# The taps of two convolution blocks as trees of accumulating DMAs, in a fused convolution and gelu kernel on one core

## The chip, the core and the metric

The kernel runs on one core of a Trainium2 chip. A core has five engines that work side by side and wait for each other through semaphores: TensorE (PE in the profile; its weight loads are the row PEld), VectorE (DVE), ScalarE (ACT), GpSimd (POOL) and SyncE (SP, which here only issues DMAs). GpSimd issues DMAs too, on a queue of its own (q0); those can add what they carry to what lies at the destination (`accum_op`). The metric is the device time of one execution in microseconds. The kernel before took 2390.29, 2388.48 and 2389.80 us in three runs, median 2389.8.

## The reference

A lightweight convolution in front of a two-layer network, all in fp32, B = 8 sequences of S = 4096 tokens, D = 192 channels. The convolution is causal and has seven taps per head; each of 8 heads has 24 channels, and its taps go through a softmax:

```
w = softmax(weight, axis=-1)                     # (8 heads, 7 taps)
out[b,s,h,:] = sum over k of w[h,k] * x_pad[b, s+k, h,:]   # six zeros ahead of x
h = out.reshape(32768, 192) @ w_in               # 192 -> 2048
g = h * (1 / (1 + exp(-1.702 * h)))
return g @ w_out                                 # 2048 -> 192
```

## The kernel before

**Steps.** The 32768 tokens are worked in 32 steps (`big`, 0 to 31). A step has 512 tokens of a sequence p and the same 512 of the sequence p + 4, so 1024 tokens. Channels lie in three blocks of 64 (`c` = 0, 1, 2); the partitions of a block hold 64 channels of two stretches of 256 tokens. Step 0 is done plainly while the weights arrive (`first_step`, `second_first`). Every other step is three stages: `hidden(big, 0)`, `hidden(big, 1)` and `second(big)`. TensorE never changes from one step to the next until it is through with all three.

**First product.** `hidden` computes `h` for half of the features (v = 0 or 1) by a scheme of 21 products (`TERMS`) in place of 24, each of a weight sum in `w_in_s` with a sum of convolution blocks. Products gather in PSUM banks (`x`, `y`, `z` among the `slots`, and `sums`), ScalarE copies some out (`copy2`, L615), VectorE combines (`sum2`, L619), and ScalarE writes the gelu to `g` (L600, L604). The weight sums `SUMS_W` are made by VectorE at the start (`sums_w_in`), and TensorE's main loop is line L578.

The convolution blocks are called C11, C12 (block 0, for the two sequences), C21, C22 (block 1) and C31, C32 (block 2). Eight sums of them, V1 to V8 (`SUMS_C`), are made by GpSimd (`sums_c`); V1 = C31 - C11 is the first. Each half of the partitions also needs the other half's blocks, so the blocks and sums cross over by DMAs on SP's queue (`cross`, L507): V1 as soon as it is there (`"first big"`), since the last-but-one stage before a step already starts its first product with V1 (`fetch`), the rest piece by piece.

**Second product.** `second` multiplies the 16 blocks of `g` by `w_out`, by a scheme of 25 products of sums of blocks with sums of weights (`w_form`). The blocks lie in "spots" of 128x1024; eight accumulations between spots are done per step by VectorE or by GpSimd's DMAs (`"acc"`, L904, 512 KB each). The results, 96x256, are combined by VectorE ("joins", L387 and L389), turned by a transpose (L846) and stored. All of it follows one list, `PLAN`, written out by hand. Its items are issued in order, each on its engine's queue: `go n` is n groups of four matmuls (L928, some 0.43 us a group; 78 in all), `main f s to` names form f, spot s and the bank where the following groups gather, `side` a form whose matmuls run as every fourth, `seed` a ScalarE copy (L957) which puts a value into a bank ahead of products that add to it, `join`, `turn` and `store` the end of a result. After the last group the stage runs on into `hidden` of the next step.

**Convolution ahead.** The blocks of a step are made two steps earlier, in two strands:

- `prepare(big)` gives items with a price in us to the queue `todo`; a call `work(us)` in `hidden` or `second_first` issues as many as fit its price. Those of block 1 are seven VectorE instructions (`conv`, L484 and L486); behind them come the sums V1 to V8 and the crossings.
- `prepare_taps(big)` gives 14 items to the queue `ready`: blocks 0 and 2, seven taps each. The seven of block 0 are issued by `("tap",)` in `PLAN`, those of block 2 by `taps_at(n)` in the v = 0 stage of `hidden`. A tap is one ScalarE multiplication and, but for the first, one GpSimd addition:

```
act.mul(home, conv_src(big, c, k), cw[:, c, k : k + 1])     # L494
nc.gpsimd.tensor_add(dst, dst, home)                        # L496, if k > 0
```

The multiplication of tap 0 writes the block itself. The others write a `home` of 128x512; there are four, half-spots of spots 16 and 15 (`TAP_SPOTS`), used in turn by both blocks. For steps 1 and 2 block 0 uses other places, since the spots are still taken.

**Order on the queues.** GpSimd takes its instructions in order: tap additions, `sums_c`, the issue of accumulating DMAs (for the DMA itself it does not wait), and at the start the weight forms: `SUMS_O` in `second_first`, and four more, `SUMS_O_LATE`, which are issued with the ScalarE sign changes `TURN_O` (L433) by `end_forms` out of `todo`, at the latest ahead of the first `second`. ScalarE takes gelus, copies, seeds and tap multiplications in order, VectorE sums, joins, turns, convolutions and the transposes of x (L465). SP issues the input loads of x (eight per step), the crossings and the stores.

Of the kernel before, what the change touches and what calls it, by code (L numbers as in the profile page):

```python
# [11 lines left out]
ALU = mybir.AluOpType  # L12
# [3 lines left out]
def kernel(  # L16
# [29 lines left out]
    nc = tc.nc  # L46

    B, S, D = x.shape
    H, K = weight.shape
# [37 lines left out]
    def load_x(big, ns=range(2)):  # L87


        p, c = divmod(big, CHUNKS)  # L90
        if c == 0 and 0 in ns:
            (nc.gpsimd if big else vec).memset(xin[0:R, :, 0, :], 0.0)
        for n in ns:
            for o in range(2):
                j = 1 if c == 0 and o == 0 else 0
                t = c * TOK + o * T + (j - 1) * Q
                for v in range(2):
                    q0 = o * R + v * Q
                    nc.sync.dma_start(
                        out=xin[q0 : q0 + Q, n, j:NJ, :],  # L100
                        in_=x_v[n, p, t : t + (NJ - j) * Q, v * Q : v * Q + XW].rearrange(
                            "(j i) d -> i j d", i=Q
                        ),
                    )
# [15 lines left out]
    def block(r, j):  # L120

        return g[:, r, j // 2, j % 2, :, :]

    def row(n, i):
        return g[:, i // NG, n, :, i % NG, :]
# [13 lines left out]
    def spot(i):  # L139

        if i >= SPOTS:
            return block(*divmod(i - SPOTS, NG))
        flat = osbs[:, i * BLK : (i + 1) * BLK] if i < 2 else room[:, ROOMS[i - 2], :]
        return flat.rearrange("p (k t) -> p k t", k=NG)

    KEPT_LATE, TAP_SPOTS = 3, (16, 15)

    def kept(i):

# [26 lines left out]
    def own(big):  # L176
        return conv_t[:, big % 2 * 2, :, :]
# [41 lines left out]
    def form(i):  # L219

        if i < WHOLE:
            return w_out_s[:, i // NG, i % NG * NG : (i % NG + 1) * NG, :]
        return w_form[:, i - WHOLE, :, :]
# [9 lines left out]
    SUMS_O_LATE = [  # L233
        (23, 1, "+", 0), (24, 1, "+", 3), (1, 14, "+", 22), (7, 0, "-", 21),
    ]
# [73 lines left out]
    for c in range(NC):  # L309
        part = sel[:, c, :].rearrange("i (h q) -> i h q", h=2)  # L310
        for sign in (1, -1):
            nc.gpsimd.affine_select(
                out=part,
                in_=part,
# [70 lines left out]
    def add_up(v, dst, a, op, b, eng=vec):  # L385
        if op == "+":
            eng.tensor_add(v(dst), v(a), v(b))  # L387
        elif op == "-":
            eng.tensor_sub(v(dst), v(a), v(b))  # L389
        elif op == "n":  # L390
            vec.scalar_tensor_tensor(
                out=v(dst), in0=v(a), scalar=-1.0, in1=v(b), op0=ALU.mult, op1=ALU.subtract
            )
        else:
            vec.tensor_scalar_mul(v(dst), v(a), -1.0)
# [30 lines left out]
    def add_forms(items):  # L426
        for dst, a, op, b in items:
            add_up(form, dst, a, op, b, eng=nc.gpsimd)

    def end_forms():  # L430
        add_forms(SUMS_O_LATE)
        for i in TURN_O:
            act.mul(form(i), form(i), -1.0)  # L433

# [32 lines left out]
            xin[:, ns, :, :].rearrange("p n j d -> p (n j) d")[:, :, c * R : c * R + Q],  # L467
        )

    taps = [spot(i)[:, k : k + 2, :] for i in TAP_SPOTS for k in (0, 2)]  # L470
    first_taps = [row(0, k) for k in (2, 3, 6, 7)]

    def tap_home(big, c, k):
        return (first_taps if big < 3 and c == 0 else taps)[(3 * c + k - 1) % len(taps)]

    def conv_src(big, c, k, ns=slice(0, 2)):
        return xts[big][:, c, ns, Q - PAD + k : Q - PAD + k + T]

    def conv(big, c, k, ns=slice(0, 2), times=vec.tensor_scalar_mul):
# [5 lines left out]
        else:  # L485
            vec.scalar_tensor_tensor(  # L486
                out=dst, in0=src, scalar=tap, in1=dst, op0=ALU.mult, op1=ALU.add
            )

    def tap(big, c, k):  # L490

        dst = own(big)[:, 2 * c : 2 * c + 2, :]
        home = tap_home(big, c, k) if k else dst
        act.mul(home, conv_src(big, c, k), cw[:, c, k : k + 1])  # L494
        if k:
            nc.gpsimd.tensor_add(dst, dst, home)  # L496

    def sums_c(big, i):
        add_up(
            lambda j: own(big)[:, place(big, j), :],  # L500
            *SUMS_C[i],
            eng=vec if big == 1 else nc.gpsimd,
        )
# [34 lines left out]
    def give(early, big):  # L538
        given[early] = big
        for what in waiting[early]:  # L540
            cross_now(early, *what)
        waiting[early].clear()
# [44 lines left out]
    def terms(big, v, slot, *ts, first=False):  # L587
        for t in ts:
            product1(slot, *TERMS[t], big, v, first)
            first = False  # L590
# [22 lines left out]
    def copy2(dst, src):  # L613
        for h in range(2):
            act.copy(bank(dst, h), bank(src, h))  # L615
# [10 lines left out]
    def hidden(big, v, x, z, y, sums, work, fetch, last=lambda: None):  # L626

        def pe(slot, *ts, first=False):  # L630
            terms(big, v, slot, *ts, first=first)

        def taps_at(n):
            for _ in range(0 if v else n):
                next_tap()

        def early(i):
            for item in EARLY_G[i] if v else ():
                sum_g(*item)


        if v:
            pe(z, 7, first=True)
            give(True, big)
        if v:
            pe(sums, 12)
            copy2(k15, sums)
            pe(x, 5, 17)
        else:
            pe(x, 5)  # L650
            pe(sums, 12)
            copy2(k15, sums)
            pe(x, 17)
            taps_at(1)
        gelu(B11, 0, v, x)
        if not v:
            pe(z, 7, first=True)
        pe(sums, 0)
        taps_at(1)
        copy2(k16, sums)  # L660
        taps_at(2)
        last()
        def turn_next():
            if big + 2 < N_BIG:
                need(f"done {big + 1}")
                turn_x(big + 2)

        early(0)
        if big == 1:
            work(3.2 if v else 1.6)  # L670

        pe(y, 6, 14, first=True)
        sum2(vec.tensor_sub, x, z, k15)
        early(1)
        if not v or big == 1:
            work(1.2)
        pe(sums, 13)
        copy2(k19, sums)
        pe(x, 2)
        copy2(k18, x)  # L680
        taps_at(2)
        pe(z, 11)
        pe(sums, 20, 10)
        sum2(vec.tensor_sub, k15, y, k19)
        gelu(B12, 0, v, sums)
        pe(x, 4)
        copy2(k20, x)
        sum2(vec.tensor_sub, k19, z, k19)
        early(2)
        if not v or big == 1:  # L690
            work(1.1)
        gelu(B22, 1, v, k19)
        gelu(B22, 0, v, k15)
        taps_at(1)
        pe(y, 8)
        pe(sums, 1, 9, first=True)
        pe(y, 15)
        if v and big == 1:
            turn_next()
        elif not v:  # L700
            work(2.2 if big > 1 else 1.1)
        sum2(vec.tensor_add, k20, k20, sums)
        sum2(vec.tensor_sub, k16, y, k16)
        gelu(B11, 1, v, k20)
        pe(x, 18)
        gelu(B21, 1, v, x)
        early(3)
        fetch()
        if not v:

            copy2(y, z)
        gelu(B21, 0, v, k16)
        if not v:
            work(1.2)
        if not v and big > 1:
            turn_next()
        pe(sums, 3, 19)
        if not v:
            work(0.7)
        sum2(vec.tensor_add, k18, k18, sums)  # L720
        return lambda: gelu(B12, 1, v, k18)
# [127 lines left out]
    def store(big, n, o=None, queues=(nc.sync,) * 3):  # L849
# [32 lines left out]
        ("go", 1), ("cross",), ("acc", 18, 14), ("go", 1), ("seed", "p1", "k1", 1), ("sum", 5, 7, "+", 15),  # L882
        ("tap",), ("go", 2), ("main", 21, 7, "p2", 0), ("go", 1), ("sum", 6, 14, "+", 6), ("go", 1), ("tap",),
        ("side", 7, 20, "k1"), ("go", 2), ("sum", 6, 6, "-", 17), ("main", 10, 14, "p0", 0), ("go", 2),
        ("tap",), ("seed", "k5", "p2", 1), ("cross",), ("join", "k10", "k10", "+", "k8"), ("go", 2),
        ("join", "p2", "p4", "+", "k3"), ("main", 8, 8, "p1", 0, 0, 2), ("go", 1),
        ("join", "k8", "k9", "+", "k5"), ("tap",), ("go", 1), ("join", "k8", "k7", "-", "k8"),
        ("main", 4, 6, "p4", 0), ("go", 1), ("turn", 1, 0, 1, "k10"), ("go", 1),
# [3 lines left out]
        ("join", "k2", "k2", "-", "k1"), ("main", 12, 18, "p3", 0), ("go", 1), ("turn", 0, 0, 0, "k7"),  # L892
        ("go", 1), ("join", "k6", "k6", "+", "p4"), ("tap",), ("go", 1), ("turn", 1, 1, 1, "k2"), ("go", 1),
        ("turn", 1, 0, 0, "k6"), ("store", 0, 0), ("main", 24, 19, "p5", 0), ("go", 2), ("final",),
        ("join", "k1", "p3", "-", "k3"), ("go", 1), ("turn", 0, 0, 1, "k1"), ("store", 0, 1), ("go", 1),
        ("join", "k2", "p2", "-", "k4"), ("turn", 0, 1, 1, "k2"), ("store", 1, 1),
        ("join", "k1", "p5", "+", "k5"), ("turn", 0, 1, 0, "k1"), ("join", "k8", "k8", "+", "k0"),
        ("turn", 1, 1, 0, "k8"), ("store", 1, 0),
    ]
# [1 line left out]
    def sum_g(dst, a, op, b=None):  # L901

        if op == "acc":
            nc.gpsimd.dma_start(out=spot(dst), in_=spot(a), accum_op=ALU.add)  # L904
        else:
            add_up(spot, dst, a, op, b)
# [79 lines left out]
    def work(us):  # L986
        while todo and todo[0][1] <= us + 0.2:
            us -= todo[0][1]
            todo.pop(0)[2]()

    def next_tap():
        if ready:
            ready.pop(0)[2]()
            while ready and ready[0][1] == 0:
                ready.pop(0)[2]()
# [39 lines left out]
    def first_step(fetch):  # L1035
# [118 lines left out]
            fetch()  # L1154

        second_first(between)
        load_x(3)
        need("sums")

# [63 lines left out]
```

## Time and profile before

| what | us |
| --- | --- |
| three runs, median (lowest, highest) | 2389.8 (2388.48, 2390.29) |
| profiled execution | 2388.73 |
| its span, from the first to the last instruction | 2387.0 |
| granted TensorE clock, mean | 0.996 |
| busy: PE / DVE / ACT / POOL | 2302.0 / 2070.8 / 1545.0 / 892.7 |
| GpSimd's tap additions (L496), 360 of 1.360 | 489.5 |
| ScalarE's tap multiplications (L494), 420 | 301.7 |
| GpSimd's sums of convolution blocks, 240 | 209.6 |
| accumulating DMAs L904, 124 of 512 KB, median from issue to landing | 5.8 |

A line of the profile names a line of the kernel, an engine, an operation, and the tiles it writes and reads. A row of groups gives the instructions of one kind with their number, total and mean time, and what ended the idle time before them; the view of waits lists who waited for whom, with total, count and mean; the timeline lists single instructions with start and duration; the table of stretches gives the busy time of each engine between two moments. The chain that ended last, followed back from the last instruction, lies on PE for 83% of the span and on DVE for 9%.

### The profile page before, as it was taken

Reading aid. Unit: us, or ns where it says so; the run is one execution under the profiler, and the core shown is the slowest. Engines: PE = TensorE matmul, PEld = TensorE weight load, DVE = VectorE, ACT = ScalarE, POOL = GpSimd, SP = SyncE. Lnnn points to the kernel's source line nnn. Section 1 sums busy time; section 2 is a strip of 40 time slices with the busy share of each in tenths; the row PEclk is TensorE's granted clock in tenths of the full one; section 3 lists DMA queues with packets and bytes.
Section 4 is the critical chain, followed back from the end, with each engine's and each line's share of the span. In section 5 each row is a group of like instructions: output and inputs, shape, how many; then the busy total and the mean of one; then the engine's idle time right before and its main releaser. Section 6 shows DMA issues by size and latency. Waiting matters only on the chain.

```text
span 2387.0 us, 60716 instructions
## 1 busy us (share of the span) xinstructions
PE 2302.0 (96%) x25238; PEld 1347.5 (56%) x25238; DVE 2070.8 (87%) x2794; ACT 1545.0 (65%) x2942; POOL 892.7 (37%) x824
## 2 busy tenths in 40 slices
PE   9889999999999999999999999999999999999999
PEld 5365555555555555555555555555555555555556
DVE  8978888888888888888988888888888888888877
ACT  7356666667666676666676666766567666667654
POOL 0634442434433344333444233443334432344400
PEclk9999999999999999999999999999999999999999
DMA  7254345543455534455434555344553345542343
GB/s 179 59 116 89 77 91 121 106 106 80 87 105 108 120 79 84 94 117 111 96 79 86 117 108 112 83 86 95 110 119 86 79 91 121 108 103 60 71 94 68
DMA packets 239362, 232.59 MB, mean 97 GB/s; under 512 B 114672, under 2 KB 198512, under 8 KB 238960
## 3 DMA queue, kind: packets, MB, share of 16 engines
q1 hardware_dynamic: 210656, 130.80, 24.1%
q0 software_dynamic: 26784, 97.53, 21.7%
q8 instruction: 198, 3.24, 0.6%
q10 hardware_dynamic: 1648, 0.39, 0.1%
q14 instruction: 76, 0.62, 0.1%
HBM read 53.15 MB, written 25.17 MB: 33 GB/s over the span
## 4 chain that ended last, share of the span: by engine, by line
PE 83%; DVE 9%; ACT 2%; issue 0%; ACTq 0%
PE slot L578 32%; PE slot L928 26%; PE sums L578 15%; PE sums L928 10%; DVE room L389 5%; DVE room L387 3%; DVE osbs L846 1%; ACT g L494 1%; DVE slot L387 1%; ACT room L957 0%; ACT room L953 0%; ACT w_out_s L433 0%; ACTq L953 0%; ACT room L615 0%; ACT w_form L433 0%
## 5 line engine op out<-in xcount | busy, mean ns | idle before, releaser
L578 PE MATMUL slot<-conv_t,w_in_s 64*128 64x512 f32 x3740 | 957.0, 595 | 16.4 <-issue 8.8
L928 PE MATMUL slot<-g,w_form 128*32 128x256 f32 x7024 | 713.2, 379 | 0.0
L496 POOL TENSOR_TENSOR conv_t<-conv_t,g 128x512 f32<-128x512 f32 x360 | 489.5, 1360 | 563.6 <-ACT g L494 548.7
L578 PEld LDWEIGHTS slot<-conv_t,w_in_s 64*128 64x128 f32 x3740 | 499.1, 187 | 351.3 <-issue 230.0
L578 PE MATMUL sums<-conv_t,w_in_s 64*128 64x512 f32 x1660 | 496.4, 594 | 0.3 <-DVE w_in_s L372 0.3
L389 DVE TENSOR_TENSOR g<-g 128x1024 f32<-128x1024 f32 x372 | 448.7, 1234 | 3.9 <-ACT g L604 0.7
L928 PEld LDWEIGHTS slot<-g,w_form 128*32 128x32 f32 x7024 | 371.3, 110 | 119.6
L604 ACT ACTIVATE g<-room 128x1024 f32<-128x1024 f32 x310 | 324.3, 1073 | 106.0 <-DVE room L619 106.0
L953 ACT COPY room<-slot 32x256 f32<-32x256 f32 x434 | 159.0, 366 | 352.0 <-PE slot L928 349.1
L928 PE MATMUL sums<-g,w_form 128*32 128x256 f32 x2648 | 369.5, 379 | 0.0
L928 PE MATMUL slot<-g,w_out_s 128*32 128x256 f32 x4080 | 319.5, 380 | 27.7 <-DVE room L387 23.5
L578 PEld LDWEIGHTS sums<-conv_t,w_in_s 64*128 64x128 f32 x1660 | 236.2, 187 | 152.1 <-issue 100.1
L904 POOL DMA_DIRECT2D g<-g x124 | 106.6, 860 | 525.7 <-DVE g L389 353.6
L494 ACT ACTIVATE g<-xt,cw 128x512 f32<-128x512 f32 x360 | 257.9, 743 | 2.2
L928 PEld LDWEIGHTS slot<-g,w_out_s 128*32 128x32 f32 x4080 | 162.1, 110 | 168.0 <-DVE room L387 30.3
L615 ACT COPY room<-slot 128x512 f32<-128x512 f32 x434 | 232.6, 611 | 31.3 <-PE slot L578 31.3
L486 DVE SCALAR_TENSOR_TENSOR conv_t<-xt,cw,conv_t 128x512 f32<-128x512 f32 (+1 forms) x210 | 223.6, 1065 | 7.8 <-ACT conv_t L484 3.0
L600 ACT ACTIVATE g<-slot 128x512 f32<-128x512 f32 x334 | 179.6, 592 | 42.5 <-PE slot L578 42.5
L953 ACT COPY room<-sums 32x256 f32<-32x256 f32 x217 | 79.4, 366 | 187.3 <-PE sums L928 185.6
L928 PEld LDWEIGHTS sums<-g,w_form 128*32 128x32 f32 x2648 | 175.5, 110 | 36.7
L928 PE MATMUL sums<-g,w_out_s 128*32 128x256 f32 x1872 | 149.2, 380 | 30.9 <-DVE room L387 26.4
L619 DVE TENSOR_TENSOR room<-slot,room 128x512 f32<-128x512 f32 x248 | 156.3, 682 | 7.5 <-ACT room L615 7.5
(182 smaller groups left out, 2773.5 us busy)
## 6 DMA issues: line engine op xcount, KB each, us to landing
g<-g POOLq DMA_DIRECT2D x124, 512.0 KB, 5.8
xin<-in_x_dram SPq DMA_DIRECT2D x240, 180.0 KB, 4.3
conv_t<-conv_t SPq DMA_DIRECT2D x180, 192.0 KB, 3.0
out_dram<-osbs SPq DMA_DIRECT2D x186, 128.0 KB, 2.4
g<-osbs POOLq DMA_DIRECT2D x31, 512.0 KB, 4.5
g<-room POOLq DMA_DIRECT2D x31, 512.0 KB, 5.8
conv_t<-conv_t SPq DMA_DIRECT2D x122, 64.0 KB, 3.6
conv_t<-conv_t SPq DMA_DIRECT2D x60, 128.0 KB, 3.5
```

The costliest lines, as they stand in the source:

```text
L389: eng.tensor_sub(v(dst), v(a), v(b))
L486: vec.scalar_tensor_tensor(out=dst, in0=src, scalar=tap, in1=dst, op0=ALU.mult, op1=ALU.add)
L494: act.mul(home, conv_src(big, c, k), cw[:, c, k : k + 1])
L496: nc.gpsimd.tensor_add(dst, dst, home)
L578: nc.tensor.matmul(slot[h], w_in_s[halves[h], a, v * P : (v + 1) * P], src, start=first, stop=True, skip_group_check=True,)
L600: act.activation(dst[:, :, h, :], src[h].rearrange("p (o t) -> p o t", o=2), AF.Gelu_apprx_sigmoid)
L604: act.activation(dst.rearrange("p o h t -> p h o t"), src.rearrange("p h (o t) -> p h o t", o=2), AF.Gelu_apprx_sigmoid,)
L615: act.copy(bank(dst, h), bank(src, h))
L619: op(*(bank(t, h) for t in (dst, a, b)))
L904: nc.gpsimd.dma_start(out=spot(dst), in_=spot(a), accum_op=ALU.add)
L928: nc.tensor.matmul(dst, w, t, start=first, stop=last, skip_group_check=True)
L953: act.copy(to, d)
```

## The change

Seven edits, all in the order or the engine of work that stays the same in its result:

1. Each tap of blocks 0 and 2 gets a home of its own (six per block, half-spots of spots 13, 16, 15 and of 14, 17, 18; other rows of `g` for block 0 of steps 1 and 2).
2. GpSimd's additions of these blocks are replaced by accumulating DMAs on GpSimd's queue, 256 KB each and six per block, which add homes in pairs: 1 += 2 after tap 2; 3 += 4 after tap 4; after tap 6: 5 += 6, 0 += 1, 3 += 5, 0 += 3, where 0 is the block itself. Block 1 stays on VectorE.
3. The four late weight forms are issued straight behind `second_first`, ahead of the input loads of step 3; the sign changes stay where they were.
4. In `hidden`, v = 0, a `work(2.0)` is added ahead of the product of `y` for all steps from 2 on, so up to three instructions of block 1 may come earlier there.
5. In the same stage one tap moves from ahead of `copy2(k16, sums)` to behind the gelus of B22.
6. In `PLAN` the seed `k5`, which copies `p2` into `k5`, moves ahead of a tap.
7. In `PLAN` the join `k2 = p2 - k4` moves ahead of the turn and the store of the result before it.

```diff
-    KEPT_LATE, TAP_SPOTS = 3, (16, 15)
+    KEPT_LATE, TAP_SPOTS = 3, {0: (13, 16, 15), 2: (14, 17, 18)}
...
     def end_forms():
-        add_forms(SUMS_O_LATE)
         for i in TURN_O:
...
-    taps = [spot(i)[:, k : k + 2, :] for i in TAP_SPOTS for k in (0, 2)]
-    first_taps = [row(0, k) for k in (2, 3, 6, 7)]
+    taps = {c: [spot(i)[:, k : k + 2, :] for i in TAP_SPOTS[c] for k in (0, 2)] for c in TAP_SPOTS}
+    first_taps = [row(0, k) for k in (6, 7, 10, 11, 14, 15)]
 
     def tap_home(big, c, k):
-        return (first_taps if big < 3 and c == 0 else taps)[(3 * c + k - 1) % len(taps)]
+        return (first_taps if big < 3 and c == 0 else taps[c])[k - 1]
...
+    DMA_TAPS = (0, 2)
+    TREE = {2: [(1, 2)], 4: [(3, 4)], 6: [(5, 6), (0, 1), (3, 5), (0, 3)]}
+
     def tap(big, c, k):
 
         dst = own(big)[:, 2 * c : 2 * c + 2, :]
         home = tap_home(big, c, k) if k else dst
         act.mul(home, conv_src(big, c, k), cw[:, c, k : k + 1])
-        if k:
+        if k and c not in DMA_TAPS:
             nc.gpsimd.tensor_add(dst, dst, home)
+            return
+        homes = [dst] + [tap_home(big, c, i) for i in range(1, K)]
+        for a, b in TREE.get(k, ()):
+            nc.gpsimd.dma_start(out=homes[a], in_=homes[b], accum_op=ALU.add)
...
         pe(sums, 0)
-        taps_at(1)
         copy2(k16, sums)
         taps_at(2)
...
         early(0)
-        if big == 1:
-            work(3.2 if v else 1.6)
+        if not v:
+            work(2.0 if big > 1 else 1.6)
+        elif big == 1:
+            work(3.2)
...
         gelu(B22, 0, v, k15)
-        taps_at(1)
+        taps_at(2)
         pe(y, 8)
...
-        ("tap",), ("seed", "k5", "p2", 1), ("cross",), ("join", "k10", "k10", "+", "k8"), ("go", 2),
+        ("seed", "k5", "p2", 1), ("tap",), ("cross",), ("join", "k10", "k10", "+", "k8"), ("go", 2),
...
         ("turn", 1, 0, 0, "k6"), ("store", 0, 0), ("main", 24, 19, "p5", 0), ("go", 2), ("final",),
-        ("join", "k1", "p3", "-", "k3"), ("go", 1), ("turn", 0, 0, 1, "k1"), ("store", 0, 1), ("go", 1),
-        ("join", "k2", "p2", "-", "k4"), ("turn", 0, 1, 1, "k2"), ("store", 1, 1),
+        ("join", "k1", "p3", "-", "k3"), ("go", 1), ("join", "k2", "p2", "-", "k4"),
+        ("turn", 0, 0, 1, "k1"), ("store", 0, 1), ("go", 1), ("turn", 0, 1, 1, "k2"), ("store", 1, 1),
...
         second_first(between)
+        add_forms(SUMS_O_LATE)
         load_x(3)
         need("sums")
```

## The prediction, made before the changed kernel was run

> **What bounds the kernel now.** I read the page first: TensorE is busy 96% of the span, so only the pieces in which it stands can be won. Then the waits of TensorE alone, from 300 us on, where all steps are alike:
>
> ```profile
> PE 2302.0 (96%) x25238; PEld 1347.5 (56%) x25238; DVE 2070.8 (87%) x2794; ACT 1545.0 (65%) x2942; POOL 892.7 (37%) x824
> ...
> PE sums L928 <- DVE room L387: 24.6, 14, 1.8
> PE slot L928 <- DVE room L387: 21.8, 13, 1.8
> PE sums L928 <- DVE slot L387: 4.1, 14, 0.3
> PE slot L928 <- DVE slot L387: 3.8, 13, 0.3
> ```
>
> Each step has two stalls, both in `second`: 0.3 us before the main product of form 4 and 1.8 us before that of form 24. Both wait for a VectorE join. Next, VectorE in time order there, for the step at 1034 us and for step 30, the last but one, whose `second` has no taps to make:
>
> ```profile
> 1060.66 0.43 DVE L387 TENSOR_TENSOR slot<-sums,room 96x256 f32<-96x256 f32 x1 [2.38 <-ACT room L957]
> 1061.00 0.93 DVE L387 TENSOR_TENSOR room<-room 96x256 f32<-96x256 f32 x1
> 1061.96 1.39 DVE L389 TENSOR_TENSOR room<-room 96x256 f32<-96x256 f32 x1
> ...
> 1065.17 0.99 DVE L387 TENSOR_TENSOR room<-room 96x256 f32<-96x256 f32 x1
> 1066.08 1.49 DVE L389 TENSOR_TENSOR room<-room 96x256 f32<-96x256 f32 x1
> ...
> 1067.86 0.37 DVE L387 TENSOR_TENSOR room<-room,sums 96x256 f32<-96x256 f32 x1
> ```
>
> ```profile
> 2304.85 0.41 DVE L387 TENSOR_TENSOR room<-room 96x256 f32<-96x256 f32 x1
> 2305.30 0.42 DVE L389 TENSOR_TENSOR room<-room 96x256 f32<-96x256 f32 x1
> ...
> 2307.56 0.42 DVE L387 TENSOR_TENSOR room<-room 96x256 f32<-96x256 f32 x1
> 2307.90 0.41 DVE L389 TENSOR_TENSOR room<-room 96x256 f32<-96x256 f32 x1
> ```
>
> The same four joins take 0.93, 1.39, 0.99 and 1.49 us beside GpSimd's tap adds (L496, 1.27 to 1.36 us each, 1058.7 to 1067.3) and 0.41 to 0.42 without: 3.1 us more. The last row of the first fence, `k6 + p4`, is what the form 24 product waits for, until 1068.23. The stage lengths show what that is worth, and two stretches of the start the rest (columns: us, then busy us and instructions of PE, PEld, DVE, ACT, POOL, clock, DMA share, GB/s):
>
> ```profile
> 1033.88:1070.15 36.27, 34.22 (x625) 19.97 (x625) 32.61 (x44) 17.99 (x42) 12.11 (x11) 1.00 0.52 108
> 1070.15:1107.14 36.99, 36.99 (x172) 21.66 (x168) 31.54 (x43) 30.42 (x51) 16.40 (x15) 1.00 0.43 90
> 2278.36:2312.16 33.80, 33.80 (x625) 20.17 (x624) 29.86 (x44) 13.18 (x34) 4.30 (x5) 1.00 0.56 116
> 97.50:107.00 9.50, 0.70 (x9) 0.11 (x1) 9.43 (x13) 3.97 (x7) 5.99 (x5) 0.64 0.29 64
> 130.70:138.00 7.30, 0.00 (x1) 0.00 (x1) 0.00 (x0) 1.46 (x4) 5.73 (x7) 0.75 0.00 0
> ```
>
> `second` takes 36.27 us with taps and 33.80 without, with the same 625 matmuls. At 97.5 TensorE waits for VectorE's sums of the input weights, six of them slowed to some 1.42 us beside tap adds; at 130.7 for ScalarE, which stands until 136.54 because two late forms are still in GpSimd's queue. The clock is at half from 100.2 to 110.4 and from 134.3 to 141.1.
>
> **The change part by part.** The sum is made against the profiled execution, 2388.73 us (span 2387.0 and 1.73 around it); the median of the runs is 1.07 higher.
>
> *Tap adds gone from GpSimd.* 12 adds a step leave, and 12 accumulating DMAs come. With the adds goes the slowing of VectorE in `second`. Worked through for 1034: form 4 starts at product 62 of 78 (0.431 us each), at 1060.6. The moved seed puts its copy ahead of a 0.72 us tap, so join `p2` ends at 1060.4 and the 0.3 stall goes. Seven joins and two turns at 0.33 to 0.45 us, each also waiting for its product, bring `k6 + p4` to its end at 1064.7; form 24 is due at 1065.8. That leaves 1.1 us to spare, so I take all of 36.27 - 33.80. The earlier join `k2` frees the bank that the next step writes three products in (due H + 2.6 us, H being that step's first matmul; ready before H). What is late next is the copy `final`, after the side copy of product 73: ready at H + 0.05. Of 29 such stages 27 are 36.27 to 36.28, the first 36.36 and one 35.19: 27 x 2.47 + 2.56 + 1.39 = 70.6 us.
>
> *The start.* The seven weight sums from 95.23 at 0.33 to 0.42 us instead of 10.1 us in all, the turn of 0.70 and six more bring the sum that TensorE waits for (the 13th, which ended at 106.82) to 100.6: 6.2 us less, and 0.3 less at half clock (3.5 us there before, 2.9 after). The form adds now follow only the first tree on GpSimd, at about 109, and cost 0.99 to 3.05 us each: done by 121 at the latest, when ScalarE asks at about 122. So the wait of 7.3 us goes, and 3.1 us at half clock with it (1.55). Together 15.3 us. The page TensorE: Matmul & The Clock Gate of the Trainium skill (Part 1) says that the clock halves only after an idle window of some 3.4 us; by that the gap left at 97.5, 3.2 us long, could pass at full clock, and the sum would be 1.4 us lower. The rows go the other way: half clock began 2.6 us after the last matmul began, so I keep it.
>
> *The tap moved in `hidden`.* In the step at 1070 a tap at 1074.70 stands ahead of the copies of `sums`, which end at 1076.41; one half of TensorE's matmuls then starts 0.2 and 0.1 us late (1076.46, 1076.99). With the tap behind them the copies end near 1075.8, before they are due at 1076.26. 0.3 us in 30 stages is 9 us. Bounds: nothing (another wait takes its place), and 0.74 a stage (22 us), since the `hidden` of step 31 lasts 35.40, which with one more product of 0.86 is 36.26 against 37.0.
>
> *Convolution block 1's adds moved.* Three VectorE instructions (0.48 and two of 0.75 us) now run in the 2.3 us in which VectorE stood before 1074.38; the transposes of x come some 1.1 us earlier and with them SP's eight input loads. Nothing: covered by that idle time.
>
> *The trees' latency.* This is the price that the trace does not show. Block 2's last tap ends at H + 15.9, and then three links follow each other on GpSimd, each issued (0.86 us) when the one before has landed: (5,6), (3,5), (0,3). Behind them in GpSimd's queue stand the eight sums of the convolution and the accumulation 8 += 0. Upper bound of a link: the accumulation of 128x1024, twice the bytes, which lands 4.4 us after its issue when it is alone. Of that 1.4 us pass until the first packet, and 4096-byte packets then take 0.34 us, eight to an engine. Lower bound: a cross of 64 KB, 1.9 us. I take 3.0: on SP's queue the fastest packets of 3072, 2048 and 1024 bytes took 121, 84 and 45 ns, in proportion to size, so eight of half size cost 1.4. The input loads run beside the last link; the accumulation of 148.09 us, beside such loads, took 5.2. With 0.9 for that the tree ends at H + 26. Sum V1 (0.75) and its cross behind SP's loads (2.6) are there at H + 29.4; TensorE needs V1 at H + 34.4. The eight sums at 0.73 to 1.0 us end by H + 34, 8 += 0 lands at H + 38.4, and VectorE first uses it at H + 39. At 3.0 us a link nothing waits; at 4.4 the cross is still in time, but 8 += 0 is 1.7 to 3.4 us late, of which VectorE's lead over TensorE there (1.4 us) covers a part. Price 0 to 2.0 us a step; I take 0, being nearer to the halved packets. The rest of the new traffic, 12 x 256 KB a step, falls into stretches with idle DMA (share 0.43 and 0.52). GpSimd's block 0 tree ends 1 to 2 us before block 2's first link and delays nobody.
>
> Sum: 2388.73 - 70.6 - 15.3 - 9 = 2293.8, and against the median **2295 us**.
>
> **The rivals.**
> 1. *Links at the price of the large accumulations (4.4 us).* 8 += 0 holds up VectorE at the start of `second`, and TensorE by 0.3 to 2.0 us a step: 2304 to 2355, say 2330. For it: the packet times of accumulations are known for one size alone. Against: proportion on the other queue.
> 2. *Slower than before: V1 late.* TensorE takes V1 at H + 34.4 in every step and would stand there. The tree has until H + 31; the gain is eaten when it ends 3.2 us later, at 6.1 us a link, and at 6.5 the stall of 4.4 us in 30 steps gives 2427. For it: accumulations that queue behind each other have a median of 5.8 us, and the last link meets eight input loads. The Trainium skill's page DMA: Bandwidth & Descriptors (Queues, rings and completion order) says that a DMA engine changes between queues only at packet ends, which would favour it; the 148.09 row bears that out with 0.9 us only. Against it: half the bytes, and no neighbour for (3,5) and (0,3).
> 3. *The joins stay late.* The stage of 33.80 us also had no taps on ScalarE; if the side copies behind taps were the cause, 57 us of the 70.6 would stay, and the time be 2352. For: join `p2` does wait for ScalarE. Against: the four slow joins are long, they do not wait.
>
> **How the numbers follow.** Forecast 0.74 (2281 to 2312: the bounds of the tap and of the clock below; half a microsecond a step of new waits above), rival 1 0.13, rival 2 0.07, rival 3 0.04, within 0.2% 0.02 (0.2% is about what a measurement of this kernel can tell). The range, 2281 to 2345, takes in the forecast and most of rival 1. Faster 0.91, same 0.02, slower 0.07.
>
> **What would show it.** Right: `second` at 33.8 to 34.0 us in every step, joins of 0.41 us at the end, no TensorE wait for VectorE, no gap of 7 us at 130, one of some 3 us at 97.5, `hidden` at 36.3 to 36.7. Wrong: a wait of TensorE for the cross of V1 at the end of `hidden`, GpSimd sums that end after H + 36, VectorE waiting for a DMA at the start of `second`, or links over 4.4 us.

## The result, and the profile after

The changed kernel took 2475.3 us (median; 2469.3 to 2484.5) against 2389.4: 1.036 times as long, interval 1.033 to 1.040. Forecast were 2295 and a gain. The profiled execution took 2469.28 us (span 2467.5). In the lines of the changed kernel the first product is L584, the matmuls of `second` L935, tap multiplications L496, tree DMAs L502, the old accumulations L911.

Who waits for whom from 300 us on (total us, times, longest), of TensorE, VectorE and GpSimd:

```profile
PE slot L935 <- DVE g L389: 51.6, 14, 4.6
PE sums L935 <- DVE g L389: 47.2, 14, 4.3
PE slot L584 <- DMA conv_t<-conv_t: 7.5, 10, 1.1
...
DVE g L389 <- DMA g<-osbs: 131.0, 28, 5.8
...
POOL conv_t L389 <- DMA conv_t<-g: 95.2, 27, 4.8
```

The old waits for joins are gone. In 28 steps TensorE now stands 3.5 us on average for a VectorE sum of `g` spots, which waits for an accumulation into `g` out of `osbs`: 8 += 0. The third line is new as well: the crossing of V1 comes late. The last shows GpSimd's sums waiting for a tree. GpSimd and VectorE in the step whose first matmul, H, is at 1028.16:

```profile
1044.22 0.86 POOL L502 DMA_DIRECT2D g<-g  x1 [4.47 <-ACT g L496]
...
1047.82 0.86 POOL L502 DMA_DIRECT2D g<-g  x1 [1.86 <-DMA g<-g]
1054.38 0.86 POOL L502 DMA_DIRECT2D conv_t<-g  x1 [5.71 <-DMA g<-g]
1058.67 1.54 POOL L389 TENSOR_TENSOR conv_t<-conv_t 128x256 f32<-128x256 f32 x2 [3.43 <-DMA conv_t<-g]
1060.29 1.42 POOL L387 TENSOR_TENSOR conv_t<-conv_t 128x256 f32<-128x256 f32 x2
1061.79 3.90 POOL L389 TENSOR_TENSOR conv_t<-conv_t 128x256 f32<-128x256 f32 x4
...
1065.93 0.85 POOL L911 DMA_DIRECT2D g<-osbs  x1
```

```profile
1066.11 1.22 DVE L389 TENSOR_TENSOR g<-g 128x1024 f32<-128x1024 f32 x1
1072.75 4.75 DVE L389 TENSOR_TENSOR g<-g 128x1024 f32<-128x1024 f32 x4 [5.42 <-DMA g<-osbs]
...
1097.25 0.41 DVE L387 TENSOR_TENSOR room<-room 96x256 f32<-96x256 f32 x1
1097.69 0.42 DVE L389 TENSOR_TENSOR room<-room 96x256 f32<-96x256 f32 x1
...
1099.93 0.42 DVE L387 TENSOR_TENSOR room<-room 96x256 f32<-96x256 f32 x1
1100.27 0.41 DVE L389 TENSOR_TENSOR room<-room 96x256 f32<-96x256 f32 x1
```

The first three rows of GpSimd are the links 5 += 6, 3 += 5 and 0 += 3 of block 2's tree. Each is issued when the one before has landed; behind the last come the eight sums, and behind these the accumulation, at H + 37.8. VectorE goes on at H + 44.6, where it was ready at H + 39.2. The four slow joins do take 0.41 to 0.42 us now; that step of the forecast came true and is drowned.

The stall does not act alone. Three stretches of this kernel (us, then busy us and instructions of PE, PEld, DVE, ACT, POOL, clock, DMA share, GB/s): two `second` stages, and 8 us inside the first of them:

```profile
1064.93:1104.52 39.59, 35.34 (x625) 19.35 (x624) 30.10 (x44) 17.94 (x41) 9.61 (x13) 0.96 0.64 126
1142.16:1179.44 37.28, 34.01 (x625) 20.09 (x624) 29.85 (x44) 17.93 (x41) 9.13 (x11) 1.00 0.67 132
1072.00:1080.00 8.00, 3.75 (x48) 1.84 (x48) 7.22 (x7) 1.08 (x3) 0.86 (x1) 0.79 0.50 109
```

From one matmul's start to the next the stall was 4.63 us in the first stage, 3.65 in the second. Of the 29 `second` stages from step 2 on, 14 have a clock of 0.96 and 9 one of 0.91 or 0.92: one or two stretches of some 3.4 us at half clock, each worth up to 1.7 us. All of them begin on one grid of 3.41 us (within 0.02 us), so what a stall costs hangs on where it falls: of two stalls of 3.81 us one left its stage at full clock, the other cost two stretches. The Trainium skill, TensorE: Matmul & The Clock Gate (Part 1), has a free-running window of 3413 ns that must pass idle for the clock to halve, so that the phase decides. The trace agrees on the phase: stalls of 3.65 to 3.81 us left four stages at full clock, others of 3.4 to 3.8 cost one or two windows. On the length it differs, and the measurement decides: stalls shorter than the window cost a stretch too, one of 3.37 us here and one of 2.38 us in e5_loads_late (in the `second` that begins at 1297.23).

Where the 80.5 us between the two spans lie, by the stages of the two traces:

| part | forecast | measured |
| --- | --- | --- |
| from the start to `second` of step 1 (154.57 to 152.72 us) | -15.3 | -1.85 |
| `second`, step 1 (36.36 to 33.81) and 29 more (mean 36.15 to 39.16) | -70.6 | +84.8 |
| `hidden`, 29 steps (mean 36.99 to 36.92) | -9 | -2.1 |
| rest | 0 | -0.3 |

The 29 `second` stages are 155 us longer than they would be at 33.81: 102 us are the stalls (99 of them in the view of waits, which starts at 300 us), and 32 half-clock stretches (14 stages with one, 9 with two), each up to 1.7 us, account for the other 53.

### The profile page after: what moved, and what is told of

Same layout as the page of the kernel before. It is cut to its first block, busy times and chain, and to the rows that moved or that the text cites. A ratio compares the mean times of both kernels' runs of the same rounds, so it can differ in the third digit from the quotient of the medians.

```text
span 2467.5 us, 61028 instructions
## 1 busy us (share of the span) xinstructions
PE 2332.5 (95%) x25238; PEld 1225.8 (50%) x25238; DVE 1886.5 (76%) x2794; ACT 1550.2 (63%) x2942; POOL 703.6 (29%) x824
## 5 line engine op out<-in xcount | busy, mean ns | idle before, releaser
L584 PE MATMUL slot<-conv_t,w_in_s 64*128 64x512 f32 x3740 | 873.1, 593 | 14.6 <-DMA conv_t<-conv_t 7.5
L935 PE MATMUL slot<-g,w_form 128*32 128x256 f32 x7024 | 710.2, 379 | 0.0
L584 PEld LDWEIGHTS slot<-conv_t,w_in_s 64*128 64x128 f32 x3740 | 390.7, 187 | 436.3 <-issue 322.6
L935 PEld LDWEIGHTS slot<-g,w_form 128*32 128x32 f32 x7024 | 368.1, 110 | 125.7
L584 PE MATMUL sums<-conv_t,w_in_s 64*128 64x512 f32 x1660 | 412.8, 592 | 9.8 <-ACT room L621 9.5
L502 POOL DMA_DIRECT2D g<-g x240 | 215.2, 909 | 652.0 <-ACT g L496 244.9
L935 PE MATMUL slot<-g,w_out_s 128*32 128x256 f32 x4080 | 336.6, 395 | 51.6 <-DVE g L389 51.6
L935 PE MATMUL sums<-g,w_form 128*32 128x256 f32 x2648 | 368.6, 379 | 0.0
L584 PEld LDWEIGHTS sums<-conv_t,w_in_s 64*128 64x128 f32 x1660 | 181.3, 187 | 187.5 <-issue 124.5
L935 PEld LDWEIGHTS slot<-g,w_out_s 128*32 128x32 f32 x4080 | 165.7, 113 | 200.4 <-DVE g L389 58.4
L496 ACT ACTIVATE g<-xt,cw 128x512 f32<-128x512 f32 x360 | 248.6, 729 | 13.5 <-DMA conv_t<-g 11.3
L502 POOL DMA_DIRECT2D conv_t<-g x120 | 122.4, 1020 | 326.3 <-DMA g<-g 164.9
L935 PE MATMUL sums<-g,w_out_s 128*32 128x256 f32 x1872 | 166.1, 413 | 50.5 <-DVE g L389 50.5
L911 POOL DMA_DIRECT2D g<-g x124 | 106.2, 856 | 347.5 <-ACT room L960 92.9
L935 PEld LDWEIGHTS sums<-g,w_form 128*32 128x32 f32 x2648 | 176.6, 110 | 38.5
L389 POOL TENSOR_TENSOR conv_t<-conv_t 128x256 f32<-128x256 f32 x180 | 156.3, 882 | 112.8 <-DMA conv_t<-g 105.8
```

Of the source, the lines that this page charges most:

```text
L502: nc.gpsimd.dma_start(out=homes[a], in_=homes[b], accum_op=ALU.add)
L584: nc.tensor.matmul(slot[h], w_in_s[halves[h], a, v * P : (v + 1) * P], src, start=first, stop=True, skip_group_check=True,)
L935: nc.tensor.matmul(dst, w, t, start=first, stop=last, skip_group_check=True)
```

## The experiments

All times are medians; the ratio is to the kernel before, with its interval.

| run | us | ratio (95%) | `hidden` mean (min to max) | `second` mean (min to max) |
| --- | --- | --- | --- | --- |
| changed kernel | 2475.3 | 1.036 (1.033 to 1.040) | 36.92 (36.25 to 37.80) | 39.16 (35.10 to 41.16) |
| e1_acc_first | 2428.8 | 1.016 (1.015 to 1.018) | 40.83 (36.25 to 43.75) | 33.84 (33.81 to 34.05) |
| e2_tree0_only | 2303.0 | 0.964 (0.962 to 0.965) | 36.55 (36.25 to 37.13) | 33.81 |
| e3_no_trees | 2333.6 | 0.977 (0.975 to 0.978) | 36.25 | 35.20 (33.81 to 35.52) |
| e4_short_tail | 2519.3 | 1.054 (1.053 to 1.056) | 44.06 (39.34 to 47.50) | 33.84 (33.81 to 34.60) |
| e5_loads_late | 2349.0 | 0.983 (0.981 to 0.985) | 36.25 | 35.90 (34.43 to 40.65) |
| e6_short_order | 2498.2 | 1.045 (1.044 to 1.047) | 38.84 (36.25 to 44.29) | 38.19 (33.81 to 41.54) |
| e7_tree0_homes | 2292.6 | 0.959 (0.958 to 0.961) | 36.59 (36.25 to 37.37) | 33.81 |
| e8_late_only | 2383.9 | 0.998 (0.997 to 0.999) | 37.00 | 36.20 (33.81 to 36.55) |
| e9_plan_undone | 2363.2 | 0.989 (0.987 to 0.990) | 36.25 | 36.20 (33.81 to 36.55) |
| e10_hidden_undone | 2354.2 | 0.985 (0.984 to 0.986) | 37.00 | 35.20 (33.81 to 35.52) |
| e11_both_orders | 2297.6 | 0.962 (0.960 to 0.963) | 36.33 (36.25 to 38.60) | 33.83 (33.81 to 34.47) |
| e12_both_homes | 2289.5 | 0.958 (0.957 to 0.959) | 36.32 (36.25 to 38.39) | 33.81 (33.81 to 34.00) |

(Means over steps 2 to 30. Step 30 has no taps to make; in e3, e8, e9 and e10 it alone is the 33.81 in the brackets.)

### The accumulation ahead of the sums

```diff
-            yield "", cost, lambda i=i: sums_c(big, i)
+            yield "", cost if big < 3 else 50.0, lambda i=i: sums_c(big, i)   # V2 to V8: not before need("all")
```

> Seven of the eight convolution sums (V2 to V8) of steps from 3 on are issued behind the accumulation 8 += 0 on GpSimd's queue instead of ahead of it; nothing else changes. Theory A (queue): the accumulation was late because it stood behind eight sums that wait for the last link of block 2's tree. It is then issued when spot 0 is there or right behind sum V1, at about 31 to 33 us into the step (38 in the changed kernel), and lands before VectorE wants it at 39. TensorE's stalls of 3.4 to 5.0 us in `second` go, and the half clock behind them; `second` takes 33.8 to 34.2 us instead of 37.3 to 41.2. `hidden` stays at 36.3 to 37.8 and the start as it is. 2310 to 2325 us against 2475. Theory B (traffic): the twelve further DMAs a step make every transfer slow, and the order on one queue matters little: stalls over 3 us stay, 2430 or more.

`second` did fall to 33.8 to 34.1 us, 154 us less in all, and yet the time fell by only 47: `hidden` grew to 40.8. TensorE's waits from 300 us on, and GpSimd in the step with H at 1018.50:

```profile
PE slot L584 <- DMA conv_t<-conv_t: 41.6, 13, 4.6
PE slot L584 <- POOL conv_t L389: 36.9, 11, 4.3
```

```profile
1044.11 0.86 POOL L502 DMA_DIRECT2D conv_t<-g  x1 [5.10 <-DMA g<-g]
1048.38 0.72 POOL L389 TENSOR_TENSOR conv_t<-conv_t 128x256 f32<-128x256 f32 x1 [3.41 <-DMA conv_t<-g]
...
1049.36 0.86 POOL L911 DMA_DIRECT2D g<-osbs  x1
```

The tree still ends at H + 30, V1 is ready at H + 30.6, and its two crossings are issued on SP at 1049.13 and 1049.64, with the 512 KB accumulation between them. The first landed in 1.92 us, the second, behind the accumulation, in 4.39; in the changed kernel, where nothing stood between, the two of the step above took 1.92 and 1.99 us, and TensorE's wait there was 1.1 us at most. (The second row names GpSimd, but V1 was long done; in these steps too TensorE went on within 0.2 us of the landing of the second crossing.) So the place in GpSimd's queue did cause the stall in `second` (theory A, for that place), but the same late tree has a second customer, and moving the first transfer pushed it against the second. The forecast of 2310 to 2325 missed that.

### Only one tree, and none

```diff
-    DMA_TAPS = (0, 2)
+    DMA_TAPS = (0,)     # e2; () in e3
```

> Block 2 goes back to GpSimd additions (with the new homes), block 0 keeps its trees: six DMAs a step instead of twelve. Theory A: block 2 has no latency any more, the sums begin some 12 us earlier, the accumulation is in time; `second` 33.8 to 34.2 us, `hidden` 36.3 to 37.0, the gap of 10 us in the start stays: 2300 to 2325. Theory B: half of the further traffic, half of the loss: about 2400 to 2440. Theory C (the new homes make other work wait): as slow as the changed kernel, over 2440.

As theory A said: `second` 33.81 in all steps, and from 300 us on the view of waits has none of TensorE. Taking block 2's six DMAs back to GpSimd turns a loss of 86 us into a gain of 87. Six DMAs less a step could also act through traffic (B); e11 below decides that.

> All blocks go back to GpSimd additions; own homes, late forms, the earlier work, the moved tap, seed and join stay. Theory A: VectorE's joins are slowed again (0.9 to 1.5 us) and the stall ahead of form 24 returns, the one of 0.3 us ahead of form 4 does not: `second` about 35.8, `hidden` 36.5 to 37.0, the wait of ScalarE at 130 gone: 2355 to 2375. Theory C: slower than before, over 2400.

Faster than either theory said, 2333.6: `hidden` is 36.25 in every step, and the stall ahead of form 24 is 1.2 us in place of 1.8. TensorE's waits, and VectorE's joins beside GpSimd's additions:

```profile
PE sums L935 <- DVE room L387: 17.2, 14, 1.3
PE slot L935 <- DVE room L387: 15.9, 13, 1.2
```

```profile
1038.47 0.99 DVE L387 TENSOR_TENSOR room<-room 96x256 f32<-96x256 f32 x1
1039.39 1.49 DVE L389 TENSOR_TENSOR room<-room 96x256 f32<-96x256 f32 x1
```

With the additions back the joins are slow again (0.41 to 0.42 without). Own homes cost nothing in the steps (theory C falls). The edits that have nothing to do with DMAs are worth 56 us together; two runs share out those in the list and in `hidden` (29.5 and 20.6 us), and the late forms, alone in a run below, bring 5.9.

### The moves in the list and in `hidden`, undone in e3

> The kernel without trees (GpSimd additions in both blocks, own homes; 2333.6 us, `second` 35.24, `hidden` 36.25), with the list's two moves undone: seed k5 behind the tap again, join k2 = p2 - k4 behind the turn and the store. Theory P: the moved seed is what took away the 0.3 us stall ahead of form 4 and made the one ahead of form 24 shorter (1.2 in place of 1.8 us), so both come back: `second` 36.2 to 36.3, 2360 to 2365. Rival (the own homes did it): `second` stays at 35.2 to 35.4, 2334 to 2340.

```diff
-        ("seed", "k5", "p2", 1), ("tap",), ("cross",), ("join", "k10", "k10", "+", "k8"), ("go", 2),
+        ("tap",), ("seed", "k5", "p2", 1), ("cross",), ("join", "k10", "k10", "+", "k8"), ("go", 2),
...                                     # and join k2 = p2 - k4 behind the turn and the store again
```

Both stalls return, and `second` is 36.27 again, as before the change: the moves are worth 1.03 us a step, and GpSimd's additions the other 1.43 down to 33.81. From 300 us on:

```profile
PE sums L935 <- DVE room L387: 24.6, 14, 1.8
...
PE sums L935 <- DVE slot L387: 4.4, 14, 0.6
```

> The kernel without trees with the two moves in `hidden` undone: a tap ahead of the copies of `sums` again, and no earlier work of 2.0 us. Theory Q: these two moves shortened `hidden` from 36.99 to 36.25 us, which come back: 2353 to 2357. Rival (the own homes did it, since the four shared ones made ScalarE wait for GpSimd): `hidden` stays at 36.25, 2333 to 2336.

```diff
         pe(sums, 0)
+        taps_at(1)
         copy2(k16, sums)
...
-        if not v:
-            work(2.0 if big > 1 else 1.6)
-        elif big == 1:
-            work(3.2)
+        if big == 1:
+            work(3.2 if v else 1.6)
...
-        taps_at(2)
+        taps_at(1)
```

`hidden` 37.00 in all steps, 2354.2: the two moves together bring 0.75 us a step. Which of the two does it was not tried.

### A tree with fewer links behind the last tap

> The tree is reshaped with as many DMAs: 1 += 2 after tap 2; 3 += 4 and 1 += 3 after tap 4; 5 += 6, 0 += 1, 0 += 5 after tap 6. Two links in a row are then left after the last tap instead of three. Theory A: the tree ends some 4 us earlier (at 26 us into the step instead of 30.5), sum V1 and its cross are in time, the eight sums end at 33 and the accumulation lands at 39: stalls of 0 to 1.5 us, none with half clock; `second` 33.8 to 35.3, `hidden` 36.3 to 36.6: 2300 to 2340. Theory B: the same traffic, so hardly a change, over 2440.

```diff
-    TREE = {2: [(1, 2)], 4: [(3, 4)], 6: [(5, 6), (0, 1), (3, 5), (0, 3)]}
+    TREE = {2: [(1, 2)], 4: [(3, 4), (1, 3)], 6: [(5, 6), (0, 1), (0, 5)]}
```

The slowest of all, 2519.3, with 33.8 us in `second` and up to 47.5 in `hidden`. ScalarE and GpSimd in the step with H at 1045.26:

```profile
1065.30 1.07 ACT L621 COPY room<-slot 128x512 f32<-128x512 f32 x2 [0.41 <-PE slot L584]
1072.68 1.08 ACT L606 ACTIVATE g<-slot 128x512 f32<-128x512 f32 x2 [6.31 <-DMA conv_t<-g]
```

```profile
1066.05 0.86 POOL L502 DMA_DIRECT2D conv_t<-g  x1 [1.90 <-DMA g<-g]
1073.05 0.86 POOL L502 DMA_DIRECT2D conv_t<-g  x1 [6.14 <-DMA conv_t<-g]
```

Home 1 lies in the part of spot 14 that the first gelu of the v = 1 stage overwrites. In this tree 0 += 1, which reads it, is late: issued at 1066.05, landed 6.47 us later, and the gelu starts at once. TensorE waits for ScalarE, 139 us in 27 waits from 300 us on.

> The tree with two links behind the last tap, with block 2's six homes in another order: the home that the gelu of B11 writes first (14, first half) is given to tap 2, whose link is first, and tap 1, whose link now comes late, gets 17. Theory A: in the short tree ScalarE stood 6.3 us because this gelu overwrites a home that the late link 0 += 1 still read. With the order changed this goes; `hidden` 36.25 to 36.9, `second` 33.8 to 34.0, the gap of 10 us in the start may stay: 2295 to 2315. Rival: sum V1 is late in place of it, since 0 += 1 and 0 += 5 run beside the input loads: 0.5 to 2 us a step, 2320 to 2350.

```diff
+    taps[2] = [spot(i)[:, k : k + 2, :] for i, k in ((17, 0), (14, 0), (17, 2), (18, 2), (18, 0), (14, 2))]
```

That gelu no longer waits, but the time is 2498: the stalls for 8 += 0 and for V1 are back. My count of the tree was wrong. With 1 += 3 put in, the chain is 3 += 4, 1 += 3, 0 += 1, 0 += 5, four links from tap 4 on. In the step with H at 805.00 they were issued at 815.74, 821.09, 825.34 and 832.29, and the last landed at H + 31.8, no earlier than in the changed kernel (H + 30.4). Neither forecast nor rival named this; as a test of a shorter tail e4 and e6 say nothing.

### The input loads away from the tree

> The changed kernel with SP's eight input loads issued behind the last crossing of `second` instead of in `hidden`, beside the last links of block 2's tree. Theory L (the loads make the tail long): without them links 3 += 5 and 0 += 3 land 1 to 1.5 us earlier each, the accumulation some 1.4 us too, as in the last two steps of the changed kernel, which have no loads and stall by 1.9 and 1.5 us. `second` 35.1 to 35.6 us, no half clock, `hidden` 36.25: 2325 to 2345. Theory T (three links in a row are too many, whatever runs beside them): stalls stay over 3 us, 2420 or more.

```diff
-                turn_x(big + 2)
+                turn_x(big + 2, later if big > 1 else None)      # no load_x here any more
...
+            if i == crosses[-1] and later:                       # behind the last ("cross",) of PLAN
+                load_x(later.pop())
```

2349.0, slightly over the forecast. `hidden` is 36.25 throughout, so V1 is in time. Without neighbours the three links of the step near 1044 landed in 3.33, 3.24 and 3.29 us after their issue; in the changed kernel they took 3.32, 6.03 and 4.21. Of the long tail 3.7 us are the loads there (theory L); over the steps the tree ends at H + 27.0 (median) instead of H + 30.4. In `second` a stall of 0.8 to 2.4 us stays in most steps, and in three steps one of over 3 us, since the accumulation still stands behind the sums and now meets the loads itself (7.49 us to land, issued at 1078.31).

### Both orders

> The changed kernel with all twelve tree DMAs, the input loads issued behind the last crossing of `second`, and sums V2 to V8 behind the accumulation 8 += 0. Theory W (two waits, for the accumulation and for V1, and the half clock behind them are the whole loss; the trees' traffic itself costs nothing): `hidden` 36.25 and `second` 33.81 in every step; 186.3 + 29 x 70.06 + 35.4 + 39.0 + 1.8 = 2294. Theory B (traffic of the trees slows the rest): stalls of some kind remain, 2310 to 2350.

The edits of e1 and e5 together, with all twelve tree DMAs. TensorE's waits from 300 to 2300 us, complete, and GpSimd in the step with H at 1026.96:

```profile
PE slot L584 <- DMA conv_t<-conv_t: 2.0, 1, 2.0
PE slot L935 <- issue: 0.3, 1, 0.3
```

```profile
1050.65 0.86 POOL L502 DMA_DIRECT2D conv_t<-g  x1 [2.92 <-DMA g<-g]
1054.02 0.73 POOL L389 TENSOR_TENSOR conv_t<-conv_t 128x256 f32<-128x256 f32 x1 [2.51 <-DMA conv_t<-g]
1056.93 0.87 POOL L911 DMA_DIRECT2D g<-osbs  x1 [2.19 <-DVE osbs L387]
```

The accumulation is issued as soon as spot 0 is there, at H + 30. 2297.6 us: within 4 us of theory W, with the trees' whole traffic. So the trees' traffic as such costs nothing here (B falls), and the loss of the change was the two waits and the half clock behind them.

### The start

The first stage of the changed kernel had a new gap of 10.1 us ahead of 120.6. Waits of the changed kernel from 105 to 122 us:

```profile
ACT g L496 <- DMA conv_t<-g: 11.3, 1, 11.3
...
PE sums L584 <- ACT room L621: 9.5, 1, 9.5
```

> Tree for block 0 alone, and for step 2 the homes of block 2 are laid where no home of step 2's block 0 lies (both use parts of 14, 17 and 18 there). Theory H (overlap): ScalarE's tap 2 of block 2 stood 11.3 us until the last link of block 0's first tree had read the home that it writes; the gap of 10.2 us in TensorE at 107 us into the first stage goes, and with it 1.7 us at half clock: 2291 to 2293, against 2303 without. Rival: ScalarE would wait for something else of the same age (GpSimd's late forms, the input loads): 2300 to 2303.

```diff
+        if big == 2 and c == 2:
+            return [spot(i)[:, k0 : k0 + 2, :] for i, k0 in ((14, 0), (17, 0), (18, 0), (15, 2), (16, 2), (13, 0))][k - 1]
```

2292.6, as theory H said; `second` of step 1 begins at 142.62 instead of 152.90. Step 2's block 0 uses rows of `g` which are the second halves of spots 13, 14, 17 and 18; block 2's tap 2 writes one of them and had to wait for the last link that reads it.

> The kernel before, with the four late weight forms issued behind `second_first` and nothing else changed. By the prediction's step the wait of 7.3 us at 130 and 1.55 us at half clock go: 2381. But the forms then run on GpSimd right behind the six tap additions at 95 to 104, and by the run without trees (gap of 11.9 us at 96 instead of 9.4) they slow VectorE's weight sums for longer, by 2.5 us: 2381 to 2385. If the forms held up the taps behind them: 2389 or more.

```diff
     def end_forms():
-        add_forms(SUMS_O_LATE)
...
         second_first(between)
+        add_forms(SUMS_O_LATE)
```

2383.9: the wait at 130 goes, and the gap ahead of 107 grows from 9.4 to 11.8 us, because the forms keep GpSimd busy beside VectorE's weight sums for longer.

> The same, and for step 2 the homes of block 2 laid clear of those of block 0. Theory W with theory H: the gap of 10 us at 108 us and 1.7 us at half clock go too: 2282 to 2285. If in the start another wait takes the place of the gap: 2290 to 2294.

e11 with the homes of e7: 2289.5, the lowest median of all (its runs overlap those of e7), though 5 us over the forecast. `second` of step 1 took 40.95 us:

```profile
140.35:181.30 40.95, 36.49 (x626) 19.75 (x625) 29.83 (x44) 17.92 (x41) 8.22 (x10) 0.92 0.75 153
```

With the gap gone, step 1, which keeps the old order of sums and loads, has the stall for 8 += 0 itself (4.5 us and a clock of 0.92). An estimate of a version which orders step 1 too, from 40.95 - 33.81: 7 us less.

## Why the prediction was wrong

- *Tap adds gone* (-70.6): right. e2 and e7 have 33.81 in every `second`, e9 and e3 share the 2.46 us out as 1.03 for the moved seed and join and 1.43 for GpSimd's additions. The forecast had given the seed 0.3 and the join nothing, so its split was off.
- *The trees' latency* (0 taken, 0 to 2.0 us a step as bounds): this step failed. Measured are 5.35 us a step. Its terms: a link was put at 3.0 us, with 0.9 more for loads beside the last one, and the tree's end at H + 26. Alone a link takes 3.3 us (e5), so that value was nearly right. But the loads start at H + 18.6 and meet the second link also, for which the forecast saw no neighbour; the three medians over 28 steps are 3.31, 5.54 and 4.28 us, and the tree ends at H + 30.4. The eight sums took 7.0 us, within the forecast (0.73 to 1.0 us each). The accumulation was to land in 4.4 us; it took 6.6 (median), beside the crossings. It landed at H + 44.2 and not at H + 38.4, so 5.0 us after VectorE was ready for it, of which TensorE stood 3.5; the half clock is the other 1.8 us a step.
- *Where the figure of 4.4 came from.* A DMA here is split over sixteen engines, and a waiter needs all of them: 3 += 5, issued at 1047.82, had its first completion after 4.36 us and its last after 6.03, at 1053.85, and the next link was issued at 1054.38. I had read the first of the sixteen completions. For the accumulation of 148.09 us the first came after 5.21 us and the last after 6.41; for the one at 1101.29 after 4.35 and 5.29. For the transfer alone this mattered little: by last completions 8 += 0 has a median of 4.5 us in the kernel before. But it hid what loads cost, 1.9 us (6.41 - 4.5) and not the 0.9 of the sum. So 4.4 was no upper bound for a link beside loads, nor for 8 += 0 beside crossings. The list of DMA issues, before and after:

```profile
g<-osbs POOLq DMA_DIRECT2D x31, 512.0 KB, 4.5
```

```profile
g<-g POOLq DMA_DIRECT2D x240, 256.0 KB, 4.2
...
conv_t<-g POOLq DMA_DIRECT2D x120, 256.0 KB, 4.8
...
g<-osbs POOLq DMA_DIRECT2D x31, 512.0 KB, 6.5
```

- *The price of a late transfer.* Rival 1 had the mechanism and the place (8 += 0 holds VectorE at the start of `second`), at 0.3 to 2.0 us a step, all of it still faster than before. The stall is 3.5 us, and in 23 of 29 stages half clock follows it, for 1.8 us a step on average. The half clock, which I had priced for the start, I did not put behind my own rivals.
- *Rival 2* (V1 late): true in the changed kernel, but small: in 17 of 28 steps 0.7 to 1.7 us passed there from one matmul's start to the next, against 0.42 undisturbed, and not 4.4 more. In four of the 17 the trace names a VectorE sum (L625) in place of the crossing. It would have become the bound with the first wait away, as e1 showed (`hidden` 40.8).
- *Rival 3* (joins late because of ScalarE's taps): false, e2.
- *The start* (-15.3): the first gap shrank from 9.39 to 3.17 us as worked out. I had kept a half clock behind it; the clock there was 1.00 (100.4 to 104.0 us), so that term, some 1.4 us, was not there. That was the phase: the same gap of 3.16 to 3.17 us stands in the profiles of nine of the kernels, and in six of them (e1, e4, e5, e6, e7, e11) a half-clock stretch of 3.4 us follows. The rule of the Trainium skill, TensorE: Matmul & The Clock Gate (Part 1), by which only an idle window of some 3.4 us halves the clock, held in three of the nine. The wait at 130 went. What I had not looked for is the overlap of homes in step 2. With it cleared (e7) the start gains 11.95 us.
- *The moves in `hidden`* (-9, bounds 0 and 22): the upper bound was right, 0.75 us a step or 21.7 us (e10). In the changed kernel 19 of these were lost again: 10 in the waits for V1, 4 in those for the VectorE sum, and for the rest the cause stays open (e2, which has no wait of TensorE, loses 9 too). Part of the 0.75 may be the earlier work, which I had costed at nothing.

## What to carry to other kernels

A chain of DMAs that wait for each other costs the landing of the slowest of its engines at every link, in the company that it really has; read the last completion, and lay the transfers of the other queues beside every link. Ask of a result that comes later not only who uses it, but what stands behind it in the same in-order queue and which memory it keeps from being overwritten: here the first was a 512 KB accumulation that had nothing to do with the trees. The saving of 2.5 us a step in `second` (1.03 of it by the two moves in the list) came whole once the order was mended: the same traffic gave 1.036 and 0.962. Block 2's trees, which had cost it all, bring little of it themselves: 2297.6 us against 2303.0 of e2, where block 2 has none, and 2289.5 against 2292.6 (e12 and e7).

## What the runs showed of the hardware

- Accumulating DMAs of 256 KB took 3.3 us alone. As the middle link of the tree one took 5.29 to 7.72 us in the 27 steps of the changed kernel with eight input loads beside it, and 3.27 and 3.23 in the two without. In e11 the 512 KB ones from `g` to `g` had a median of 9.3 us beside loads (5.8 in the kernel before), and no wait of TensorE came of it.
- A small transfer was slow behind a large one of another queue: V1's second crossing of 64 KB took 4.39 us with a 512 KB accumulation issued 0.28 us ahead of it, and its twin 0.5 us earlier 1.92 (e1). In 18 steps of e1 whose landings the trace has, the second took 4.37 to 5.10 us and the first 1.92 to 2.06.
- The four runs of the changed kernel differ by 15 us, those of e2 by 0.6. With stalls near 3.5 us it hangs on the phase whether each costs 0, 1.7 or up to 3.4 us more. That is not the whole spread: the slowest of the four had a clock of 0.969 against 0.975 of the fastest, but two with 0.974 lie 9 us apart.
- Two corrections to the text ahead of the prediction: of the sums of spots, six a step are accumulating DMAs (186 in 31 steps), and the others are VectorE's; and the third number in a row of waits is the longest, not the mean.
